# A kernel of attention and mixture of experts on one core: in VectorE's program for the experts, the part for units of one half block stands first behind the test of the unit's size

## The chip, the cores and the metric

The kernel runs on one core of a Trainium2 chip. The metric is the device time of one execution in microseconds (us); of several executions the median is taken. The engines are TensorE (PE in the profile, PEld for its weight loads), VectorE (DVE), ScalarE (ACT), GpSimd (POOL) and SyncE (SP), which here issues most of the DMAs. Each engine runs its own row of instructions; a "q" behind the name (DVEq) means the engine's sequencer, which takes branches and waits on semaphores.

## The reference

The first half is attention over keys and values averaged in groups of eight; the second half gives each of 4608 tokens to the one expert of eight that its gate likes best.

```python
def _attn_ref(q, k, v):                       # q, k, v: 8 x 8 heads x 576 x 64
    k_p = k.reshape(B, H, Sp, pool, D).mean(axis=3)
    v_p = v.reshape(B, H, Sp, pool, D).mean(axis=3)
    scores = scale * np.matmul(q, k_p.transpose(0, 1, 3, 2))
    ...
    return np.matmul(attn, v_p).astype(np.float32)

def _moe_ref(x, w_gate, w1, w2):              # x: 4608 x 512, w1: 8 x 512 x 1024, w2: 8 x 1024 x 512
    logits = x @ w_gate
    expert_idx = np.argmax(logits, axis=1)
    ...
    for e in range(E):
        mask = expert_idx == e
        xe = x[mask]
        h = np.maximum(xe @ w1[e], 0.0)
        out[mask] = gate_w[mask, None] * (h @ w2[e])
```

## The kernel before

Attention runs first and writes each token's row to a buffer of its expert in device memory. `plan` then works out a table from the counts of tokens. `experts` goes through that table unit by unit: a unit is up to 512 tokens of one expert, counted in half blocks of 64 tokens (`n`, 1 to 8, the table's column K_U). With the inputs at hand there are 13 units, 0 to 12, with 8, 8, 1, 6, 4, 8, 5, 8, 4, 1, 8, 8 and 6 half blocks. Units 2 and 9 have one half block. K_SW is 1 for a unit that begins a new expert, here for units 2, 3, 4, 5, 7, 9 and 10; the weights change there.

The matrix products are done in parts of high and low precision. ScalarE rounds an operand to the high part and VectorE takes the difference as the low part: `whi` (L1161) and `wlo` (L1169) for a piece of the weights W, eight pieces of 128x1024 per expert, 0 to 3 of W1 and 4 to 7 of W2, which SyncE loads into ST (L1427); `xhi` (L1123) and `xlo` (L1137) for the tokens X; `hhi` (L1059) and `hlo` (L1080) for the hidden values H, in eight groups f = 0 to 7 per unit. PE multiplies X with W1 in eight groups (L888) and H with W2 (L946).

A unit of one half block has its own form: PE multiplies with tokens as the fixed side (L913) and turns the result back (L924); ScalarE takes the rows (`htake`, L1038) and the high part (`hhi1`, L1048); VectorE sums halves (`hsums`, L1044) and takes the low part (`hlo1`, L1052), twice each (a = 0 and 1). PE's L946 for the first four k waits for `hlo1(u, 0)`, that for the last four for `hlo1(u, 1)`.

Nothing is scheduled by a tool in `experts`. Each engine's program is written out by hand for up to 16 units, with tests of `n` and of K_SW at run time; the engines meet at semaphores. For a unit VectorE runs `hidden_lo` (L1208 on: the low parts of H, with the W2 pieces between) and then `following`, which branches on `n` again (L1316, L1319); for one half block it runs `hlo1(u, 1)` and then, in `next_part` (test of K_SW at L1246), `xlo` and the W1 pieces of the next unit. After that come the unit's outputs Y (L1302 to L1308) and the table reads for the unit after the next (`keep`). The test values `n` and K_SW stand in registers that `keep` loaded a unit earlier.

SyncE loads for each unit, in this order: X of the unit after the next (L1392), its gates (L1384), the W2 pieces of the unit's expert to come (`stage(u, 1)`, L1427; after a unit of one or two half blocks only when PE has finished with its outputs, L1451), and the W1 pieces (`stage(u + 1, 0)`).

Of the kernel before, what the change touches and what calls it, by code (L numbers as in the profile page):

```python
# [47 lines left out]
K_U, K_SW, K_ROW, K_ST, K_AH, NK = 0, 1, 2, 6, 7, 8  # L48
# [3 lines left out]
def f32(a):  # L52
    return a.bitcast(F32)
# [684 lines left out]
def experts(ctx, tc, xs, w1v, w2v, out, tab, W, ident, empty, scr, u0, banks):  # L738
# [14 lines left out]
    pe, act, dve, sp, pool = nc.tensor, nc.scalar, nc.vector, nc.sync, nc.gpsimd  # L753

    with tc.tile_critical():
# [10 lines left out]
        def entry(eng, a, u, lo, hi):  # L766
            r = regs.get((eng, a, u))
            return eng.value_load(tab[u : u + 1, a : a + 1], min_val=lo, max_val=hi) if r is None else r
# [43 lines left out]
        def col(eng):  # L812
            c = next(cols[eng])
            return scr[:, c : c + 1]
# [5 lines left out]
        def vnop(n, v):  # L820
            dve.tensor_copy(out=col(dve), in_=scr[:, 0:1]).then_inc(Q[n], v)
# [76 lines left out]
        def tbank(u, a):  # L898
            return pH[(8 * u + (2, 0)[a]) % 3]

        def sums_h(u, a):

            return (hbank(u, 1) if a else pY[:, 0])[:, 0:256].rearrange("p (f t) -> p f t", f=4)
# [136 lines left out]
        def hsums(u, a):  # L1040
            dve.wait_ge(Q["P_h"], 8 * u + 4 + 4 * a)
            if a == 0:
                dve.wait_ge(Q["V_y"], 4 * u)
            dve.tensor_reduce(out=sums_h(u, a), in_=tbank(u, a).rearrange("p (f a t) -> p f t a", f=4, a=2), axis=AX.X, op=ALU.add).then_inc(Q["V_1"], 4)  # L1044
# [5 lines left out]
        def hlo1(u, a):  # L1050
            dve.wait_ge(Q["A_h"], 8 * u + 6 + 2 * a)
            dve.scalar_tensor_tensor(out=HH[:, 4 * a : 4 * a + 4, 64:128], in0=sums_h(u, a), scalar=0.0, in1=f32(HH[:, 4 * a : 4 * a + 4, 0:64]),  # L1052
                                     op0=ALU.max, op1=ALU.subtract).then_inc(Q["V_h"], 4)
# [109 lines left out]
        def wlo(u, i, other=None):  # L1163
            n, eng, q = "s1" if i < 4 else "s2", other or dve, "V_"
            eng.wait_ge(Q["A_" + n], 4 * (u - 1) + i % 4 + 1)
            if other:
                eng.wait_ge(Q[q + n], 4 * (u - 1) + i % 4)
            o = slice((i % 4) * 1024, (i % 4 + 1) * 1024)
            eng.tensor_tensor(out=(W1L if i < 4 else W2L)[:, o], in0=ST[:, i, :], in1=f32((W1H if i < 4 else W2H)[:, o]), op=ALU.subtract).then_inc(Q[q + n], 1)  # L1169

        def hidden(eng, u, part, wpart, nop, fs=range(8), small=False, turns=lambda: None):


            at = (0, 1, 3, 4) if small else (0, 1, 2, 3) if eng is act else (0, 2, 4, 6)
            for f in fs:
                part(f)
                if f == 5:
                    turns()
                if u > 0 and f in at:
                    with eng.If(entry(eng, K_SW, u, 0, 1) == 1):  # L1180
                        wpart(u, 4 + at.index(f))
                    if f == at[0]:
                        with eng.Else():
                            nop()
# [23 lines left out]
        def hidden_lo(u, fs=range(8), small=True):  # L1208
            go = lambda n, odd=None: hidden(dve, u, lambda f: hlo(u, f, n, odd), wlo, lambda: vnop("V_s2", 4), fs, n <= 2, turns if n > 2 and u > 0 else lambda: None)
            n = entry(dve, K_U, u, 1, 8)  # L1210

            def turns():
                more(dve, u + 1, lambda: [xturn(u + 1, s) for s in range(2)])

            def large():
                with dve.If(n % 2 == 0):
                    go(8)
                with dve.Else():
                    go(7, 64 * nc.s_assert_within(n, 1, 7, skip_runtime_bounds_check_because="an odd number of at most eight") - 64)

            if not small:
                return large()
            with dve.If(n > 2):
                large()
            with dve.Else():
                with dve.If(n > 1):
                    go(2)
                with dve.Else():
                    with dve.If(entry(dve, K_SW, u, 0, 1) == 1):
                        wlo(u, 4)  # L1230
                        wlo(u, 5)
                        hsums(u, 0)
                        wlo(u, 6)
                        hlo1(u, 0)
                        hsums(u, 1)
                        wlo(u, 7)
                    with dve.Else():
                        vnop("V_s2", 4)
                        hsums(u, 0)
                        hlo1(u, 0)  # L1240
                        hsums(u, 1)

        def next_part(eng, u, xf, xnop, wf, wnop, turn=None, mid=lambda: None, between=2, first=None):

# [47 lines left out]
        def dve_unit(u):  # L1292
# [58 lines left out]
            if u > 0:  # L1351
                hidden_lo(u)
# [317 lines left out]
```

## Time and profile before

| | |
|---|---|
| runs before | median 595.34 us (594.51 to 596.46, 3 runs) |
| profiled execution | 599.22 us, of which the span from the first to the last instruction is 597.6 us |
| mean granted clock of PE in it | 0.993 of full speed |
| busy, share of the span | PE 95%, DVE 62%, ACT 40%, POOL 29% |
| instructions in the trace of DVE | 738 |
| unit 2 | about 262 to 273 us |
| unit 9 | about 461 to 477 us |

The profiled execution is 3.9 us longer than the median of the runs. The granted clock is the rate that PE was given as a share of 2.4 GHz: 0.50 is 1.2 GHz. In the chain of work that ended last, "issue" is time in which an engine waited for nothing that the profile shows.

### The profile page before, as it was taken

The page shows a single profiled execution, that of the slowest core. Times are in us where ns is not written, and L with a number is a line of the kernel's source. Part 1 is how long each engine was busy: PE and PEld are TensorE (multiplying, and loading weights), DVE is VectorE, ACT ScalarE, POOL GpSimd, SP SyncE. Part 2 cuts the span into 40 slices and gives each one's busy share as a digit, 9 for nine tenths or more (in the row PEclk, how much of TensorE's full clock was granted, in tenths as well). Part 3 has the DMA queues.
Part 4 walks back from the last instruction along what each step waited for, and adds up shares of the span by engine and source line. Part 5 has one row for each costly group of instructions (what it writes and reads, how often), then busy time and mean ns, then how long its engine had stood idle before and what let it go on. Part 6 is the DMA issues. An engine that isn't in the chain of part 4 may idle for free.

```text
span 597.6 us, 13333 instructions
## 1 busy us (share of the span) xinstructions
PE 565.0 (95%) x4332; PEld 500.6 (84%) x4332; DVE 373.3 (62%) x738; ACT 240.7 (40%) x445; POOL 171.0 (29%) x250
## 2 busy tenths in 40 slices
PE   6988998999998999999998999999999799999995
PEld 5777987979877888888997889878898688888994
DVE  6698787888785223648959662786338768234221
ACT  2566675688531112346544420434125642021110
POOL 7456666556343111124211101030112220101101
PEclk9999999999999999999999999999999799999999
DMA  8979989797422557456685953044513542100101
GB/s 320 367 226 287 287 258 282 198 278 187 126 107 90 163 159 246 146 162 219 147 298 132 319 164 112 2 149 145 177 40 119 132 162 58 57 0 21 55 4 55
DMA packets 93946, 96.54 MB, mean 162 GB/s; under 512 B 43102, under 2 KB 74846, under 8 KB 93792
## 3 DMA queue, kind: packets, MB, share of 16 engines
q1 hardware_dynamic: 85808, 74.27, 43.4%
q0 software_dynamic: 7440, 20.50, 9.5%
q8 instruction: 60, 0.98, 0.7%
q14 instruction: 94, 0.77, 0.4%
q10 hardware_dynamic: 544, 0.02, 0.1%
HBM read 72.68 MB, written 26.00 MB: 165 GB/s over the span
## 4 chain that ended last, share of the span: by engine, by line
PE 66%; DVE 11%; issue 9%; SPq 4%; POOL 4%; DMA 3%; ACT 2%; DVEq 1%; POOLq 0%; ACTq 0%
PE pU L946 26%; PE pP L888 16%; PE pq L888 8%; PE pU L322 4%; PE pP L306 2%; DMA XE<-in_v_dram 2%; POOL dispatched L431 2%; PE pS L286 2%; PE pq L276 2%; PE pP L488 2%; DMA ST<-in_moe_w_dram 1%; DVE mx L290 1%; SPq L1392 1%; POOL raw L195 1%; SPq L1427 1%
## 5 line engine op out<-in xcount | busy, mean ns | idle before, releaser
L946 PE MATMUL pU<-W,H 128*128 128x512 f32 x912 | 203.7, 384 | 5.3 <-DVE H L1052 3.2
L946 PEld LDWEIGHTS pU<-W,H 128*128 128x128 f32 x912 | 173.4, 191 | 31.9 <-DVE H L1052 3.4
L1504 POOL DMA_INDIRECT out_dram<-Y,GT x51 | 55.6, 1091 | 308.2 <-DVE Y L1308 226.7
L888 PE MATMUL pP<-X,W 128*128 128x512 f32 (+3 forms) x660 | 122.0, 340 | 3.8 <-DVEq L1544 1.5
L888 PEld LDWEIGHTS pP<-X,W 128*128 128x128 f32 x660 | 108.4, 190 | 14.1 <-issue 3.3
L1059 ACT ACTIVATE H<-pP 128x512 fp32r<-128x512 f32 x56 | 33.4, 597 | 143.4 <-PE pP L888 135.4
L1308 DVE TENSOR_SCALAR Y<-pU,GT 128x512 f32<-128x512 f32 x36 | 26.8, 749 | 86.6 <-PE pU L946 78.7
L1080 DVE SCALAR_TENSOR_TENSOR H<-pP,H 128x512 fp32r<-128x512 f32 (+1 forms) x62 | 39.9, 643 | 53.9 <-ACT H L1059 50.6
L1169 DVE TENSOR_TENSOR W<-ST,W 128x1024 fp32r<-128x1024 f32 x54 | 64.2, 1213 | 9.0 <-ACT W L1161 8.5
L1161 ACT CAST W<-ST 128x1024 fp32r<-128x1024 f32 x56 | 56.8, 1051 | 27.1 <-PE pU L946 20.0
L888 PE MATMUL pq<-X,W 128*128 128x512 f32 (+3 forms) x324 | 62.4, 342 | 0.0
L322 PE MATMUL pU<-V,pt 110*128 110x146 f32 (+3 forms) x468 | 56.7, 283 | 1.4 <-ACT pt L307 0.8
L888 PEld LDWEIGHTS pq<-X,W 128*128 128x128 f32 x324 | 53.8, 190 | 5.0 <-issue 0.2
L322 PEld LDWEIGHTS pU<-V,pt 110*128 110x128 f32 (+3 forms) x468 | 51.4, 179 | 3.1 <-ACT pt L307 1.6
L431 POOL DMA_INDIRECT dispatched<-xe,ix x36 | 39.8, 1105 | 17.2 <-POOL ix L392 7.3
L1059 ACT ACTIVATE H<-pq 128x512 fp32r<-128x512 f32 x28 | 16.7, 598 | 61.1 <-PE pq L888 60.0
L1132 DVE STREAM_TRANSPOSE pS<-XE 128x512 f32<-128x512 f32 x26 | 38.0, 1503 | 0.0
L307 ACT COPY pt<-pP 110x384 f32<-110x384 f32 x72 | 30.7, 479 | 6.1 <-PE pP L306 5.7
L290 DVE TENSOR_REDUCE mx<-pS 128x8 f32<-128x576 f32 x36 | 27.1, 753 | 9.2 <-PE pS L286 4.4
L1080 DVE SCALAR_TENSOR_TENSOR H<-pq,H 128x512 fp32r<-128x512 f32 (+1 forms) x30 | 19.6, 655 | 20.5 <-ACT H L1059 19.5
L299 ACT ACTIVATE P<-sd 128x576 f32<-128x576 f32 x36 | 24.8, 689 | 17.8 <-DVE sd L293 16.1
L306 PE MATMUL pP<-ident,P 128*110 128x128 f32 x216 | 30.0, 275 | 0.6 <-ACT P L299 0.6
(205 smaller groups left out, 610.9 us busy)
## 6 DMA issues: line engine op xcount, KB each, us to landing
ST<-in_moe_w_dram SPq DMA_DIRECT2D x56, 512.0 KB
raw<-in_k_dram SPq DMA_DIRECT2D x12, 768.0 KB
raw<-in_v_dram SPq DMA_DIRECT2D x11, 768.0 KB
XE<-dispatched SPq DMA_DIRECT2D x104, 64.0 KB, 2.2
qa<-in_q_dram SPq DMA_DIRECT2D x24, 256.0 KB
w<-in_moe_w_dram SPq DMA_DIRECT2D x8, 512.0 KB
XE<-dispatched SPq DMA_DIRECT2D x15, 256.0 KB, 4.0
qa<-in_q_dram SPq DMA_DIRECT2D x2, 1024.0 KB
```

The costliest lines, as they stand in the source:

```text
L290: nc.vector.tensor_reduce(out=mx, in_=s4, axis=AX.X, op=ALU.max)
L306: nc.tensor.transpose(pPs[a][0:R, c * P : (c + 1) * P], Ps[t % 2][:, o : o + R], ident)
L322: nc.tensor.matmul(pu[p0 : p0 + n, a, h * VW : (h + m) * VW], lhsT=pt[t][a][0:r, c % 3 * P + p0 : c % 3 * P + p0 + n], rhs=Vs[g % 2][0:r, ...
L431: apart(nc.gpsimd.indirect_dma_start(out=xs, out_offset=bass.IndirectOffsetOnAxis(ap=at, axis=0), in_=rows, in_offset=None))
L888: r = pe.matmul(out=pH[g % 3][:, :m], lhsT=w1s(w, f, k), rhs=x, start=i == 0, stop=i == len(passes) - 1)
L946: r = pe.matmul(out=pY[:, s % 2, :], lhsT=h, rhs=in_turn(w[:, k * 512 : (k + 1) * 512]), start=start and i == 0, stop=stop and i == len(ps ...
L1059: act.activation(out=HH[:, f, o], in_=src[:, o], func=AF.Relu).then_inc(Q["A_h"], 1)
L1080: return dve.scalar_tensor_tensor(out=dst[:, f, to], in0=src[:, at], scalar=0.0, in1=f32(HH[:, f, at]), op0=ALU.max, op1=ALU.subtract)
L1132: dve.transpose(out=pX[:, s % 2, :].rearrange("p (c a g t) -> p c g t a", c=4, a=2, g=4), in_=XE[u % 2][:, s, :].rearrange("p (g r c) -> p ...
L1161: act.copy(out=(W1H if i < 4 else W2H)[:, o], in_=ST[:, i, :]).then_inc(Q["A_s1" if i < 4 else "A_s2"], 1)
L1169: eng.tensor_tensor(out=(W1L if i < 4 else W2L)[:, o], in0=ST[:, i, :], in1=f32((W1H if i < 4 else W2H)[:, o]), op=ALU.subtract).then_inc( ...
L1504: pool.indirect_dma_start(out=out, out_offset=bass.IndirectOffsetOnAxis(ap=GT[:, u, s, 1:2].bitcast(I32), axis=0), in_=Y[:, s, :], in_offs ...
```

## The change

In `hidden_lo` the two tests of the unit's size change places. Before, `n > 2` is tested first (L1223), the larger units' part stands behind it, then the part for two half blocks (test L1226), then that for one half block (test of K_SW at L1229). After, `n < 2` is tested first (L1223), with the one-half-block part directly behind it (test of K_SW at L1224), and then `n > 2` (L1238), the larger units' part and the part for two half blocks. The parts themselves are the same, and so are the programs of the other engines. VectorE's program has 6697 built instructions in both.

```diff
-            with dve.If(n > 2):
-                large()
+            with dve.If(n < 2):
+                with dve.If(entry(dve, K_SW, u, 0, 1) == 1):
+                    wlo(u, 4)
+                    wlo(u, 5)
+                    hsums(u, 0)
+                    wlo(u, 6)
+                    hlo1(u, 0)
+                    hsums(u, 1)
+                    wlo(u, 7)
+                with dve.Else():
+                    vnop("V_s2", 4)
+                    hsums(u, 0)
+                    hlo1(u, 0)
+                    hsums(u, 1)
             with dve.Else():
-                with dve.If(n > 1):
+                with dve.If(n > 2):
+                    large()
+                with dve.Else():
                     go(2)
-                with dve.Else():
-                    with dve.If(entry(dve, K_SW, u, 0, 1) == 1):
-                        wlo(u, 4)
...
-                    with dve.Else():
-                        vnop("V_s2", 4)
...
```

VectorE's row for unit 9 before, at the end of the parts for larger units, where the one-half-block part begins (L1064 and L1080 belong to the part for two half blocks):

```order
L1080 SCALAR_TENSOR_TENSOR H<-pP_65,H 128x128
L1080 SCALAR_TENSOR_TENSOR H<-pP_66,H 128x128
L1226 UNCONDITIONAL_BRANCH
L1229 COMPARE_AND_BRANCH
L1169 TENSOR_TENSOR W<-ST,W 128x1024 x2
L1044 TENSOR_REDUCE pU<-pq 128x256
L1169 TENSOR_TENSOR W<-ST,W 128x1024
L1052 SCALAR_TENSOR_TENSOR H<-pU,H 128x4x64
L1044 TENSOR_REDUCE pP_66<-pP_65 128x256
L1169 TENSOR_TENSOR W<-ST,W 128x1024
L1229 UNCONDITIONAL_BRANCH
```

VectorE's row for unit 9 after, from the end of unit 8 (L1367; L783 is the test whether there is a unit 9) through the test of the size:

```order
L1367 UNCONDITIONAL_BRANCH
L783 COMPARE_AND_BRANCH
L1223 COMPARE_AND_BRANCH
L1224 COMPARE_AND_BRANCH
L1169 TENSOR_TENSOR W<-ST,W 128x1024 x2
L1044 TENSOR_REDUCE pU<-pq 128x256
L1169 TENSOR_TENSOR W<-ST,W 128x1024
L1052 SCALAR_TENSOR_TENSOR H<-pU,H 128x4x64
L1044 TENSOR_REDUCE pP_66<-pP_65 128x256
L1169 TENSOR_TENSOR W<-ST,W 128x1024
L1224 UNCONDITIONAL_BRANCH
```

The one-half-block part has moved from 108 rows behind the test L1223 to the row directly behind it, ahead of the larger units' part (some 86 built instructions) and of that for two half blocks (some 31). Its end branch was a few rows ahead of the join; it now passes both other parts.

VectorE's row for unit 2 after, at the join behind `hidden_lo`, where `following` begins (before, the first three rows are the end of the one-half-block part):

```order
L1064 TENSOR_REDUCE pq<-pq 128x128
L1080 SCALAR_TENSOR_TENSOR H<-pP_66,H 128x128
L1080 SCALAR_TENSOR_TENSOR H<-pq,H 128x128
L1240 UNCONDITIONAL_BRANCH
L1316 COMPARE_AND_BRANCH
L1246 COMPARE_AND_BRANCH
L1137 TENSOR_TENSOR X<-pS,X 128x8x64 x2
```

VectorE's row for unit 2 further on, in both kernels at the same place: the part of `following` for one half block, which L1316 and L1319 lead to (L1249 ends the part for two half blocks).

```order
L1169 TENSOR_TENSOR W<-ST,W 128x1024 x4
L1249 UNCONDITIONAL_BRANCH
L1052 SCALAR_TENSOR_TENSOR H<-pq,H 128x4x64
L1246 COMPARE_AND_BRANCH
L1137 TENSOR_TENSOR X<-pS,X 128x8x64 x2
L1112 COMPARE_AND_BRANCH
L1137 TENSOR_TENSOR X<-pm,X 128x8x64
```

Nothing moved between L1316, L1319 (91 rows behind L1316) and these rows (34 behind L1319); what changed is where VectorE comes from: before, from six rows ahead of L1316 in unit 2, after, from 109 rows ahead of it.

## Rows read from the trace of the kernel before

**Rows 1.** The page of the profiled execution, whole program: the span, the busy line of the engines, the granted clock in 40 slices, and the DMA queue of kind instruction (packets, MB, share).

```profile
span 597.6 us, 13333 instructions
...
PE 565.0 (95%) x4332; PEld 500.6 (84%) x4332; DVE 373.3 (62%) x738; ACT 240.7 (40%) x445; POOL 171.0 (29%) x250
...
PEclk9999999999999999999999999999999799999999
...
q14 instruction: 94, 0.77, 0.4%
```

**Rows 2.** What PE's queue waited for: the first row from 455 us to the end, the other two from 262 to 460 us. Columns: engine, line, what was waited for, us in total, times, longest us.

```profile
PE pU L946 <- DVE H L1052: 3.2, 1, 3.2
...
PE pP L888 <- DVE X L1137: 1.4, 1, 1.4
...
PE pU L946 <- DVE W L1169: 0.5, 1, 0.5
```

**Rows 3.** The chain of work that ended last, 455 to 490 us, through unit 9. Columns: start us, duration us, what (DVEq is VectorE's sequencer).

```profile
461.32 0.06 DVEq L1223
...
461.52 0.06 DVEq L1226
461.58 4.61 issue
...
466.20 0.05 DVEq L1229
...
466.30 0.13 DVE W L1169
...
470.02 0.05 DVEq L1229
...
470.79 6.51 PE pU L946 x16
```

**Rows 4.** Stretches of 2 us: busy time of each engine, then PE's granted clock, the DMA share and GB/s.

```profile
458.00:460.00 2.00, 2.00 (x11) 1.76 (x10) 2.00 (x3) 0.00 (x0) 0.00 (x0) 1.00 0.94 302
...
468.00:470.00 2.00, 0.00 (x0) 0.00 (x0) 2.00 (x3) 0.38 (x1) 0.00 (x0) 0.91 0.35 67
...
470.00:472.00 2.00, 1.21 (x3) 1.04 (x4) 2.00 (x4) 1.81 (x4) 0.20 (x1) 0.50 0.46 112
...
474.00:476.00 2.00, 2.00 (x6) 1.62 (x5) 2.00 (x3) 2.00 (x3) 0.72 (x1) 0.50 0.37 81
...
476.00:478.00 2.00, 2.00 (x10) 1.66 (x9) 2.00 (x3) 0.29 (x1) 0.00 (x0) 0.88 0.17 14
...
266.00:268.00 2.00, 1.98 (x17) 1.74 (x16) 1.93 (x3) 2.00 (x5) 0.00 (x0) 1.00 0.12 41
```

**Rows 5.** VectorE's branches by line, the first five in unit 2 (261 to 274 us), the last at the start of a later unit (288 to 294 us). Columns: line, operation, count, duration in ns, first and last start in us.

```profile
L1226 DVEq COMPARE_BRANCH  x1: 62/62/62, 262.5 to 262.5; - x1
...
L1229 DVEq COMPARE_BRANCH  x2: 47/48/50, 262.6 to 267.5; - x2
...
L1316 DVEq COMPARE_BRANCH  x1: 56/56/56, 267.7 to 267.7; - x1
...
L1319 DVEq COMPARE_BRANCH  x1: 56/56/56, 268.2 to 268.2; - x1
...
L1246 DVEq COMPARE_BRANCH  x1: 56/56/56, 268.8 to 268.8; - x1
...
L1246 DVEq COMPARE_BRANCH  x1: 63/63/63, 290.3 to 290.3; - x1
```

**Rows 6.** VectorE's line of time, 268 to 273.2 us (unit 2) and 288 to 294 us (the last row). Columns: start us, us, engine, line, operation, what, count, and in brackets the idle time before it and what ended it.

```profile
269.22 0.42 DVE L1052 SCALAR_TENSOR_TENSOR H<-pq,H 128x256 fp32r<-128x256 f32 x1
...
270.68 1.29 DVE L1137 TENSOR_TENSOR X<-pS,X 128x512 fp32r<-128x512 f32 x2 [1.04 <-ACT scr L818]
...
272.49 0.14 DVE L821 COPY scr<-scr 128x1 f32<-128x1 f32 x1
...
292.90 1.29 DVE L1137 TENSOR_TENSOR X<-pS,X 128x512 fp32r<-128x512 f32 x2 [0.24 <-issue]
```

**Rows 7.** Lines of time around unit 9's end and unit 10, columns as in rows 6: PE's last transposes of unit 9's stretch, ScalarE's first casts of it, SyncE's loads, then ScalarE, VectorE and PE at unit 10's fifth group.

```profile
466.96 0.65 PE L840 MATMUL pU<-ident,XE 128*128 128x128 f32 x4
...
461.01 1.99 ACT L1161 CAST W<-ST 128x1024 fp32r<-128x1024 f32 x2 [4.62 <-PE pU L946]
...
464.55 10.06 SPq L1392 DMA_DIRECT2D XE<-dispatched  x16
475.26 2.75 SPq L1384 DMA_DIRECT2D GT<-dispatched  x4
480.75 2.92 SPq L1427 DMA_DIRECT2D ST<-in_moe_w_dram  x4
...
484.46 1.04 ACT L1161 CAST W<-ST 128x1024 fp32r<-128x1024 f32 x1 [3.94 <-DMA ST<-in_moe_w_dram]
...
486.68 0.68 DVE L1080 SCALAR_TENSOR_TENSOR H<-pP,H 128x512 fp32r<-128x512 f32 x1
...
487.49 2.78 PE L888 MATMUL pP<-X,W 128*128 128x512 f32 x12
```

**Rows 8.** The chain of work that ended last, 476 us to the end. Columns as in rows 3.

```profile
575.81 15.55 PE pU L946 x72
591.36 0.02 issue
```

More of the change, by code (lines that the diff above doesn't have):

```diff
@@ L1222, in hidden_lo @@
                 return large()
-            with dve.If(n > 2):
-                large()
+            with dve.If(n < 2):
[12 more added lines that the diff above has]
+                    hsums(u, 1)
             with dve.Else():
-                with dve.If(n > 1):
+                with dve.If(n > 2):
+                    large()
+                with dve.Else():
                     go(2)
-                with dve.Else():
-                    with dve.If(entry(dve, K_SW, u, 0, 1) == 1):
-                        wlo(u, 4)
[L1231 to L1236, printed above, removed]
-                    with dve.Else():
-                        vnop("V_s2", 4)
-                        hsums(u, 0)
-                        hlo1(u, 0)
-                        hsums(u, 1)
         def next_part(eng, u, xf, xnop, wf, wnop, turn=None, mid=lambda: None, between=2, first=None):
```

## The prediction

> **What bounds the kernel.** The page gives TensorE (PE) 95% busy in a span of 597.6 us and the clock near full almost everywhere [rows 1]. So a change on VectorE (DVE) counts only where PE waits for it, or where PE's waiting takes its clock down. I read PE's waits next, for the two stretches that hold the one-half-block units: unit 2 (about 262 to 273 us) and unit 9 (461 to 477 us). After 455 us PE waits once, 3.2 us for H of line 1052, which is `hlo1` of unit 9; its waits from 262 to 460 are small ones for DVE, the longest 1.4 us [rows 2]. The other units take the branch to a larger part, before and after.
>
> The chain through unit 9 shows what `hlo1` was late for [rows 3]: DVE runs the tests L1223 and L1226 within 0.2 us, and then nothing until L1229, 4.61 us later, called "issue". L1229 is a branch on a register that was loaded a unit earlier; it waits for no semaphore. What can be late is the instruction itself. PE's last transposes end at 467.6; it then stands until 470.79 [rows 3, 7]. The stretches show what followed [rows 4]: the granted clock is 0.91 in 468–470, 0.50 in 470–476 (1.2 GHz), 0.88 in 476–478. PE's 16 matmuls L946 take 6.51 us [rows 3]; at full clock 72 of them take 15.55 us [rows 8], so 16 take 3.46. Unit 9 thus loses about 3.2 us to the wait and up to 3.05 us to the clock.
>
> In unit 2 the same jump, L1226 to L1229, shows no hole (262.5 to 262.6 [rows 5]), so the distance alone costs nothing; whether the code is already there decides. It is late elsewhere too [rows 5, 6]: L1246 runs at 290.3 and the L1137 behind it not before 292.90, 2.6 us later, put down to "issue"; in unit 2 L1319 runs at 268.2, L1246 at 268.8, and L1137 at 270.68, after 1.04 us idle put down to a ScalarE copy, 2.45 us behind L1319. My reading: DVE's code comes in pieces (94 packets of kind instruction, 0.77 MB on one queue, 8.2 KB each [rows 1]), one piece is asked for when DVE enters the one before it, and it takes 2.4 to 2.9 us, or 4 to 5.3 us where the DMA share is near 1 (0.94 in 458–460, against 0.12 in 266–268 [rows 4]). Counting built instructions, I place the edges 128 instructions apart; that count is inference, the holes are rows.
>
> The Trainium skill, page "Runtime: NRT & Kernel Launch", section "Instruction fetch mechanics", says that prefetch is sequential and normally hidden, and that a taken branch to a target outside a two-line window stalls on a fetch. By that rule only far jumps stall; the trace disagrees, since 290.3 to 292.90 is a step to the next piece with no far jump, and by the rule the change would cost unit 2 nothing.
>
> **The change, step by step.**
>
> *Larger units.* One more branch, L1238, jumps over some 21 instructions. Near branches stand 0.2 us apart [rows 3]; ten units times 0.2 us lie on DVE's sequencer while PE works ahead, so 0 on the path; 0.2 us each at each of the two waits for DVE shown in [rows 2] where a larger unit begins, if the cover is gone: 0.4 us at most.
>
> *Where the small part lies now.* It stands directly behind L1223, in the piece already there: no hole at its start. But its end jump L1224 now passes the larger parts (some 126 instructions) into the next piece, and L1316, two branches later, jumps on to L1319, into the piece behind, which is asked for only then. The hole moves from ahead of the small part to behind it, ahead of `hlo1(u, 1)` and of `xlo`, the low half of the next unit's X.
>
> *Unit 2* had no hole ahead of the small part, so it can only lose. The part itself is held by W pieces and by PE's transposes and ends where it did, about 267.5. L1316 comes at about 268.0, after the jump into a ready piece (0.5 us, as from L1316 to L1319 before). L1319 waits for its piece, 2.45 us: 270.5, was 268.2. `hlo1` follows at about 270.8, was 269.22; the next piece is asked for at 270.5 and `xlo` starts at 273.0, was 270.68: +2.35. From `xlo` to PE's next unit the chain is DVE's own (L1137, L821 at 272.49 [rows 6], PE next), so unit 3 starts 2.35 us late. Behind it PE waits 1.4 and 0.5 us for DVE [rows 2]; these waits end by the same late chain, so I let them absorb 0.3. Unit 2: +2.05 us. Bounds: 0 if the piece is hidden, 2.8 if both fetches take 2.9 us and nothing absorbs.
>
> *Unit 9* gets rid of the 4.61 us. The small part starts when ScalarE has rounded W2's first piece, about 462.1 (the first of two casts from 461.01 [rows 7]), instead of 466.30; its W pieces, sums and `hlo1(9, 0)` keep their spacing (3.7 us from 466.30 to the end branch at 470.02 [rows 3], plus waits for PE's transposes), so it ends at about 466.7 and L1316 runs at 467.3. Now L1319's piece is asked for at about 467, with the DMA share down to 0.35 in 468–470 [rows 4]: 2.5 to 3 us, 469.8. `hlo1(9, 1)` runs at about 470.1 to 470.8; `xlo` at 470.5 to 473.2. PE starts L946 at 467.6 with two pauses of about 1 us and no fall of the clock, and reaches unit 10 at about 473.7 instead of 477.1: −3.4 us. Bounds: 0 if the new fetch takes 5.3 us, −4.2 without a second hole.
>
> *What unit 10 does with it* is where I expect the gain to go. PE's fifth group of unit 10 starts at 487.49, directly behind DVE's H at 486.68, which takes up what ScalarE's H writes behind ScalarE's W at 484.46; that W had waited 3.94 us for a W2 load [rows 7]. The load belongs to four that SyncE issues from 480.75 on, in its own sequence: behind 16 loads of X from 464.55 and the gate loads from 475.26, with table reads between [rows 7]; from 461 to 489 the waits of SyncE's queue show none. ScalarE takes its instructions in order, so its H for the fifth group stands behind that W piece. With unit 10 begun 3.4 us earlier, PE finishes its first four groups at 484.1 and stands until about 487.45: 3.4 back to 0. That pause is as long as the one in unit 9 before, behind which the clock stayed at 0.50 until about 476.5, 5.7 us after PE's restart; the same in unit 10 costs 2.8 us of work. Bounds 0 to 2.8; I take 2.1, nearer to the row, since whatever lengthens unit 9's second hole shortens this pause. From there PE runs without a pause to 591.4 [rows 8], so what is lost stays lost. If the W2 load is not what holds the fifth group, the 3.4 us stay.
>
> Sum: unit 2 +2.05, unit 9 −3.4, unit 10 +3.4 +2.1, larger units 0: +4.1 us. The profiled execution took 599.2 us (span 597.6 and 1.6 around it), 3.9 above the median of the runs, 595.34; differences carry over, so 595.3 + 4.1 = 599.4 us.
>
> **Rivals.**
>
> *PE waits in unit 10, but the clock stays up.* 595.3 + 2.05 = 597.4. For it: PE pauses of up to 1.4 us left the clock alone; against it: the pause expected is 3.3 us, as in unit 9.
>
> *The clock falls in unit 2 too.* There PE would stand twice, about 1.3 and 1.9 us, around eight matmuls. The only fall in the rows came about 2 us into a pause. It adds up to 2.8: 602.0.
>
> *The new holes are hidden.* If VectorE's code is always there one piece and more ahead, and only the 4.61 us were a far jump's, unit 2 loses nothing, unit 9 gains, unit 10 takes the gain back. Without a clock loss 595.3; with it 597.4. The holes behind 290.3 and 268.8 speak against it. This is what the rule of the Trainium skill's page above would make of the change.
>
> *Not slower: unit 10 isn't held.* If DVE and ScalarE, coming earlier, have the fifth group's H ready without that W2 piece (or SyncE's loads come earlier with the unit), PE keeps the 3.4 us: 595.3 + 2.05 − 3.4 = 594.0, and under 593.5 where unit 2 loses less than 1.6. It decides from the point where ScalarE's W leaves 484.46: if that moves with unit 10, this case holds. Against it: SyncE's order depends on none of what moves.
>
> **Chances.** About 0.3%, 1.8 us, is what a measurement of this kernel can tell from no change. Forecast (599.4, from 598 to 600.3): 0.46. No clock loss in unit 10 (597.4): 0.18. Clock falls in unit 2 too (602): 0.08. Holes hidden (595.3 to 597.4): 0.13. Unit 10 not held (594.0): 0.15. Slower by over 0.3% (above 597.1): the first and third whole, two thirds of the second, under a third of the fourth: 0.68. Faster (under 593.5): 0.10, half of the last case and some of the fourth. Same: 0.22. The range from 593.6 to 600.8 leaves out the case with two clock losses, the better half of the last, and the upper edge of the forecast's. The forecast's own range is 598.0 to 600.3.
>
> **What would show it.** In the changed profile the hole L1223 to L1224 in unit 9 is gone; L1316 to L1319 shows 2.4 us or more in units 2 and 9; unit 2's L1137 comes 5.0 us behind L1316 (3.0 before), and PE waits some 2 us there; the clock row has its low slice in unit 10, not in unit 9; ScalarE's W still waits for a W2 load at unit 10's fifth group. If L1319 follows L1316 by 0.5 us in unit 2, the piece count is wrong; if the low slice is gone altogether, the clock term is.

## The result and the profile after

The changed kernel takes 600.77 us (median of 6 runs, 600.0 to 602.19) against 596.53 us for the kernel before, in the same comparison: ratio 1.0077, 95% interval 1.0053 to 1.0100. That is 4.6 us, 3.2 to 6.0. A second comparison gave 601.42 us and 1.0092 (1.0061 to 1.0123), 5.5 us. The forecast was +4.1 us and 599.4, from 598.0 to 600.3; both measured times lie above that range, the first just inside the wider one that ends at 600.8. As a difference +4.1 lies inside both intervals (3.2 to 6.0 and 3.6 to 7.3 us). The kernel before took 1.2 us more in this comparison than the 595.34 that the forecast was built on.

The page of the profiled execution of after, to be laid beside [rows 1]:

```profile
span 598.3 us, 13341 instructions
...
PEclk9999999999999999999999999999999989999999
```

The low slice of the granted clock has moved one place to the right, from the end of unit 9 to unit 10. What PE's queue waited for, the first three rows from 262 to 460 us, the other two from 455 us to the end (columns as in [rows 2]):

```profile
PE pP L888 <- DVE W L1169: 3.0, 1, 3.0
PE pP L888 <- DVE scr L821: 1.7, 1, 1.7
PE pU L946 <- DVE H L1052: 1.4, 1, 1.4
...
PE pP L888 <- DVE H L1080: 3.5, 1, 3.5
PE pU L946 <- DVE H L1052: 2.1, 1, 2.1
```

Before, there were 3.2 us for `hlo1` of unit 9 and little else. Now `hlo1` costs 1.4 us in unit 2 and 2.1 in unit 9, the start of unit 3 another 1.7, the start of unit 5 3.0 (1.4 before) and the fifth group of unit 10 3.5. VectorE's branches, the first three in unit 2, the other four in unit 9 (columns as in [rows 5]):

```profile
L1224 DVEq COMPARE_BRANCH  x1: 47/47/47, 261.6 to 261.6; - x1
...
L1316 DVEq COMPARE_BRANCH  x1: 56/56/56, 262.1 to 262.1; - x1
...
L1319 DVEq COMPARE_BRANCH  x1: 56/56/56, 264.7 to 264.7; - x1
...
L1223 DVEq COMPARE_BRANCH  x1: 43/43/43, 459.2 to 459.2; - x1
...
L1224 DVEq COMPARE_BRANCH  x2: 43/45/47, 459.3 to 464.6; - x2
...
L1316 DVEq COMPARE_BRANCH  x1: 63/63/63, 465.2 to 465.2; - x1
...
L1319 DVEq COMPARE_BRANCH  x1: 63/63/63, 467.6 to 467.6; - x1
```

In unit 9 the test of K_SW (L1224) follows L1223 in 0.1 us, where before 4.61 us passed ahead of it [rows 3]. In both units L1319 now stands 2.4 to 2.6 us behind L1316, where it was 0.5. VectorE's line of time in unit 2 (columns as in [rows 6]):

```profile
264.99 0.42 DVE L1052 SCALAR_TENSOR_TENSOR H<-pq,H 128x256 fp32r<-128x256 f32 x1 [1.58 <-issue]
267.14 1.29 DVE L1137 TENSOR_TENSOR X<-pS,X 128x512 fp32r<-128x512 f32 x2 [1.73 <-issue]
...
268.95 0.14 DVE L821 COPY scr<-scr 128x1 f32<-128x1 f32 x1
```

`hlo1` and `xlo` each stand behind a hole put down to "issue". L1137 comes 5.0 us behind L1316, 3.0 before [rows 5, 6]. In unit 10 (SyncE, ScalarE and PE, lines of time; answers to [rows 7]):

```profile
462.71 11.32 SPq L1392 DMA_DIRECT2D XE<-dispatched  x16
...
479.25 2.70 SPq L1427 DMA_DIRECT2D ST<-in_moe_w_dram  x4
...
483.46 1.04 ACT L1161 CAST W<-ST 128x1024 fp32r<-128x1024 f32 x1 [7.67 <-DMA ST<-in_moe_w_dram]
...
472.33 2.83 PE L888 MATMUL pq<-X,W 128*128 128x512 f32 x12 [1.06 <-DVE W L1169]
...
486.42 7.13 PE L888 MATMUL pP<-X,W 128*128 128x512 f32 x24 [3.49 <-DVE H L1080]
```

PE's fifth group waits 3.49 us for the H that stands behind ScalarE's W, which waited for the W2 load issued at 479.25. Stretches of 2 us behind it (columns as in [rows 4]):

```profile
484.00:486.00 2.00, 0.00 (x0) 0.00 (x0) 1.47 (x2) 1.90 (x3) 0.00 (x0) 1.00 1.02 391
486.00:488.00 2.00, 1.58 (x7) 1.38 (x8) 1.69 (x3) 2.00 (x5) 0.00 (x0) 0.94 0.44 169
488.00:490.00 2.00, 2.00 (x7) 1.53 (x6) 1.09 (x2) 1.00 (x2) 0.00 (x0) 0.50 0.47 101
490.00:492.00 2.00, 2.00 (x8) 1.68 (x7) 0.71 (x2) 0.60 (x1) 0.00 (x0) 0.71 0.55 125
```

The clock falls to 0.50 here as it did in unit 9 before: the 24 matmuls of L888 take 7.13 us instead of 5.34.

To see where the time went, the executions are cut where PE starts on a unit (its first L913 or L888, or the first L946 of unit 10), two traces of each kernel. For the first trace of before these starts are 192.14, 261.55, 272.73, 327.69, 460.75, 477.13 and 497.88 us, and PE ends at 591.35; for the first of after 185.93, 255.65, 269.19, 325.65, 458.64, 472.33, 498.57 and 592.03. Us:

| stretch | before | before, again | after | after, again | mean difference | forecast |
|---|---|---|---|---|---|---|
| units 0 and 1 | 69.41 | 69.74 | 69.72 | 69.36 | 0.0 | 0 |
| unit 2 | 11.18 | 12.30 | 13.54 | 14.13 | +2.1 | +2.35 |
| units 3 and 4 | 54.96 | 54.17 | 56.46 | 54.14 | +0.7 | −0.3 |
| units 5 to 8 | 133.06 | 133.09 | 132.99 | 134.16 | +0.5 | 0 |
| unit 9 | 16.38 | 15.92 | 13.69 | 12.38 | −3.1 | −3.4 |
| unit 10, to its first L946 | 20.75 | 21.70 | 26.24 | 28.84 | +6.3 | +5.5 |
| the rest | 93.47 | 93.47 | 93.46 | 93.46 | 0.0 | 0 |
| sum | 399.21 | 400.39 | 406.10 | 406.47 | +6.5 | +4.1 |

The first L888 of unit 0 starts at 192.14 us in the first trace of before and between 185.9 and 187.2 in the other three: attention and the plan differ by that much between executions of one code. The stretches behind them differ too, by 1.2 us in sum between the two traces of before. So four traces and the medians agree only to about 2 us.

### The profile page after: what moved, and what is told of

It reads as the page before. It is cut to its first block, busy times and chain, and to the rows that moved or that the text cites. A ratio compares the mean times of both kernels' runs of the same rounds, so it can differ in the third digit from the quotient of the medians.

```text
span 598.3 us, 13341 instructions
## 1 busy us (share of the span) xinstructions
PE 564.2 (94%) x4332; PEld 499.9 (84%) x4332; DVE 372.3 (62%) x738; ACT 240.6 (40%) x445; POOL 171.3 (29%) x250
## 4 chain that ended last, share of the span: by engine, by line
PE 67%; DVE 15%; issue 6%; SPq 3%; DMA 3%; ACT 2%; DVEq 2%; POOL 1%; POOLq 0%; ACTq 0%
PE pU L946 27%; PE pP L888 17%; PE pq L888 8%; PE pU L322 4%; PE pP L306 2%; DMA XE<-in_v_dram 2%; DVE mx L290 2%; PE pS L286 2%; DVE sd L293 2%; PE pP L488 2%; SPq L1392 2%; DVE raw L195 2%; DVE W L1169 2%; PE pm L230 1%; PE pq L276 1%
## 5 line engine op out<-in xcount | busy, mean ns | idle before, releaser
L946 PE MATMUL pU<-W,H 128*128 128x512 f32 x912 | 201.4, 380 | 5.1 <-DVE H L1052 3.5
L946 PEld LDWEIGHTS pU<-W,H 128*128 128x128 f32 x912 | 171.2, 189 | 31.5 <-issue 5.4
L888 PE MATMUL pP<-X,W 128*128 128x512 f32 (+3 forms) x660 | 123.7, 344 | 9.8 <-DVE H L1080 3.7
L888 PEld LDWEIGHTS pP<-X,W 128*128 128x128 f32 x660 | 109.6, 191 | 20.9 <-issue 5.4
L1080 DVE SCALAR_TENSOR_TENSOR H<-pP,H 128x512 fp32r<-128x512 f32 (+1 forms) x62 | 39.9, 643 | 56.3 <-ACT H L1059 54.5
L888 PE MATMUL pq<-X,W 128*128 128x512 f32 (+3 forms) x324 | 62.5, 343 | 1.2 <-DVE W L1169 1.1
L888 PEld LDWEIGHTS pq<-X,W 128*128 128x128 f32 x324 | 53.7, 190 | 6.7 <-issue 1.9
L1080 DVE SCALAR_TENSOR_TENSOR H<-pq,H 128x512 fp32r<-128x512 f32 (+1 forms) x30 | 19.6, 654 | 20.3 <-ACT H L1059 19.7
L195 POOL TENSOR_TENSOR raw<-raw 128x768 f32<-128x768 f32 (+1 forms) x18 | 27.1, 1504 | 10.9 <-DMA raw<-in_v_dram 10.2
```

The lines of the kernel that those rows point to most:

```text
L195: return lambda: eng.tensor_tensor(out=out, in0=raw[:, :, 0:n], in1=raw[:, :, n : 2 * n], op=ALU.add)
L888: r = pe.matmul(out=pH[g % 3][:, :m], lhsT=w1s(w, f, k), rhs=x, start=i == 0, stop=i == len(passes) - 1)
L946: r = pe.matmul(out=pY[:, s % 2, :], lhsT=h, rhs=in_turn(w[:, k * 512 : (k + 1) * 512]), start=start and i == 0, stop=stop and i == len(ps ...
L1080: return dve.scalar_tensor_tensor(out=dst[:, f, to], in0=src[:, at], scalar=0.0, in1=f32(HH[:, f, at]), op0=ALU.max, op1=ALU.subtract)
```

## The experiments

The theory: VectorE's code comes in pieces of 128 instructions, one asked for ahead, so that the change moves a hole from ahead of unit 9's small part to behind both small parts; unit 2 pays, and what unit 9 gains unit 10 gives back behind a late W2 load, with the clock on top. The rivals: the loss is unit 2's alone; the holes belong to one execution; unit 10 is held by VectorE's or ScalarE's work. Ratios are to the kernel before in the same comparison. Some of the kernels have a few lines more, so that L946 is L947 there, L888 is L889, L1316 is L1332.

**The two units apart.** In the first run the new order stands in unit 9 alone, in the second in unit 2 alone:

```diff
-            with dve.If(n < 2):
-                ...
+            if u in FIRST:        # (9,) in the first run, (2,) in the second
+                with dve.If(n < 2):
+                    ...           # the order of the change
+            else:
+                with dve.If(n > 2):
+                    ...           # the order of before
```

> The order of the change for unit 9 alone; every other unit as before. Theory (code comes in pieces; unit 2 and unit 9 pay apart): unit 2 is as before, L1316 to L1319 stands 0.5 us apart there; unit 9 has no hole ahead of its small part and a new one of about 2.4 us between L1316 and L1319; unit 10 starts about 2.7 us earlier against unit 9's first transposes, PE then waits about 3.5 us for the fifth group's H behind a W2 load, the clock falls there, and the end is 2 to 3 us later than before: ratio 1.003 to 1.005. Rival (the loss is all unit 2's): ratio 0.995 to 1.000.

> The order of the change for unit 2 alone. Theory: L1316 to L1319 takes about 2.5 us in unit 2 instead of 0.5, L1137 starts about 2.4 us later against PE's transposes, unit 3 starts 2.35 us late; unit 9 is as before with its 4.6 us hole and the low clock behind it. Ratio 1.003 to 1.006 (2 to 3.8 us: the upper end if PE's wait of 3.0 us ahead of unit 5 comes with it). Rival (the new holes come from how attention's end falls in a run, not from the order): L1319 0.5 us behind L1316, ratio 1.000.

Unit 9 alone: 1.0034 (1.0005 to 1.0062), 2.0 us. Unit 2 alone: 1.0045 (1.0021 to 1.0068), 2.7 us. Together 4.7, the change 4.6, with intervals of 1.4 to 1.7 us to either side of each. So both pay, and nothing else has to. VectorE's branches in unit 2, new order there (these lines are L1316 and L1319 of before):

```profile
L1332 DVEq COMPARE_BRANCH  x1: 63/63/63, 262.5 to 262.5; - x1
...
L1335 DVEq COMPARE_BRANCH  x1: 62/62/62, 265.2 to 265.2; - x1
```

The hole is 2.7 us; unit 2 takes 13.60 us. In unit 9 alone, PE's line of time:

```profile
482.89 5.45 PE L889 MATMUL pP<-X,W 128*128 128x512 f32 x24 [0.62 <-DVE H L1081]
```

Unit 9 takes 14.12 us instead of 16.38, as expected, but in this trace the fifth group waits only 0.62 us and unit 10, begun at 471.54, takes 21.81 us, not 25 or more. SyncE's W2 loads left at 475.95 here, 4.4 us behind the unit's start, in the trace of after 6.9 us behind it; the 16 loads of X ahead of them took 9.27 us to issue here and 11.32 there. What unit 10 gives back depends on when SyncE gets to these loads, and that varies; the measured 2.0 us is the answer over 12 runs. Unit 2 took 13.15 us in this trace though its order is that of before; PE stood 1.8 us ahead of L946 there, "issue", of which more below.

**The W2 loads first.** The third run is the changed kernel with SyncE's order turned in unit 9, the sixth the kernel before with the same, the fifth the new order in unit 9 alone with it:

```diff
             def following():
...
+                if u in (9,):
+                    stage(u, 1)
+                    rows()
+                    return stage(u + 1, 0)
                 rows()
                 if u > 0:
                     stage(u, 1)
```

> The changed kernel, and SyncE issues in unit 9 the W2 loads for unit 10 ahead of the X loads for unit 11. Theory (unit 10's fifth group is held by the W2 load that SyncE issues late): the loads leave at about 473 instead of 479 us, PE's wait of 3.5 us in unit 10 and the low clock behind it are gone; 4 to 5 us less than the changed kernel, ratio to before 0.998 to 1.003. Rival (the group is held by VectorE's or ScalarE's own work, the load is only the last name): PE still waits over 2 us there, ratio 1.006 to 1.010.

> The order of the change for unit 9 alone, and in unit 9 SyncE's W2 loads for unit 10 ahead of the X loads for unit 11. Theory (unit 9's part of the change gains about 3 us, the late W2 load takes them back): unit 10 starts 3 us earlier against the start of unit 9 and PE no longer waits at its fifth group; 2 to 4.5 us less than before, ratio 0.993 to 0.997. Rival (unit 9 gains nothing in most executions): ratio 0.998 to 1.003.

> The kernel before, with SyncE's W2 loads of unit 9 ahead of the X loads for unit 11 and nothing else. Theory (before, unit 10's fifth group was only just held by the load): no difference beyond 1 us, ratio 0.998 to 1.002, PE reaches unit 10 as before, 20.5 to 21 us from its start to its first L946. Rival (the order of loads alone is worth what the third experiment gained): ratio 0.990 to 0.994.

| | SyncE as before | W2 loads first in unit 9 |
|---|---|---|
| order of before | 1 | 0.9976 (0.9954 to 0.9999) |
| new order in unit 9 | 1.0034 (1.0005 to 1.0062) | 0.9939 (0.9920 to 0.9959) |
| new order everywhere | 1.0077 (1.0053 to 1.0100) | 0.9990 (0.9965 to 1.0015) |

The new order in unit 9 loses 0.34% with SyncE as before and gains 0.37% (0.9976 to 0.9939) with the loads moved. This is the point on which the rival "unit 10 isn't held" turned, and it is settled: the W2 load is what holds unit 10. SyncE and PE in the third run:

```profile
473.60 2.89 SPq L1427 DMA_DIRECT2D ST<-in_moe_w_dram  x4
480.20 8.49 SPq L1392 DMA_DIRECT2D XE<-dispatched  x16
...
484.10 5.34 PE L888 MATMUL pP<-X,W 128*128 128x512 f32 x24
```

The loads leave at 473.60 and PE goes through unit 10, begun at 473.66, without a wait, 20.79 us to its first L946; the stretches from 484 on show the clock at 1.00. The load order alone was worth a little more than expected, 1.4 us where I had allowed 1. The kernel before had something to gain there: in the four traces with unit 9 and SyncE as before unit 10 takes 20.75 to 22.03 us, and in three of them its fifth group waits 0.3 to 1.0 us for the same H; in all five with the loads moved it takes 20.7 to 20.8. The fifth run takes 592.39 us against 595.62 and is 0.6% faster than the kernel before, the lowest ratio in this study (the eleventh run's lies inside its interval). PE in its unit 9 and unit 10:

```profile
465.72 2.83 PE L947 MATMUL pU<-W,H 128*128 128x512 f32 x12 [1.83 <-issue]
469.11 2.83 PE L889 MATMUL pq<-X,W 128*128 128x512 f32 x12 [0.56 <-issue]
...
479.55 5.34 PE L889 MATMUL pP<-X,W 128*128 128x512 f32 x24
```

**One piece more in the jump.** In the fourth run 128 instructions that no unit here executes stand in unit 2's part for two half blocks, in the kernel before:

```diff
                     with dve.If(n > 1):
                         go(2)
+                        for _ in range(128 if u == 2 else 0):
+                            dve.drain()
```

> The kernel before with 128 instructions, one piece, put into unit 2's part for two half blocks, which no unit here runs: nothing more is executed, the code behind keeps its place against the pieces' edges, and the jump from L1226 to L1229 in unit 2 is one piece longer. Theory (only the next piece is asked for ahead): a hole of 2.4 to 3 us between L1226 and L1229 in unit 2, where it was 0.2; unit 3 starts 2 to 2.5 us late, ratio 1.003 to 1.005. Rival (code is there two pieces ahead, or the jump is what costs nothing at any length): no hole, ratio 1.000.

VectorE's small part of unit 2, and PE behind it:

```profile
260.11 2.36 DVE L1170 TENSOR_TENSOR W<-ST,W 128x1024 fp32r<-128x1024 f32 x2 [2.69 <-issue]
...
264.60 5.42 PE L947 MATMUL pU<-W,H 128*128 128x512 f32 x16 [1.56 <-DVE H L1053]
269.85 4.06 PE L889 MATMUL pP<-X,W 128*128 128x384 f32 x24
```

The hole is there, 2.69 us ahead of the first W piece; before there was none [rows 5]. PE waits 1.56 us for `hlo1`, the granted clock falls behind the wait (0.78, 0.50 and 0.87 in 264–270), and unit 2 takes 13.38 us instead of 11.18 and 12.30. Yet the time is 1.0003 (0.9982 to 1.0024), below the 1.003 expected: in the trace the part behind attention is 401.54 us long, 1.7 more than the mean of the two traces of before, of which unit 2 is 1.6, but the 12 runs leave room for no more than 1.4 us. The place of the hole is shown, its price in the whole is not.

That the holes are code which comes late can be read from the traces themselves, for they time every packet of queue q14 [rows 1], 8192 bytes each. Here one ends at 258.55 and L1229 of before runs at 260.01, 1.5 us later. In unit 2 of the changed kernel packets end at 263.32 and 265.78; L1319 and `xlo` follow 1.4 us behind them. In unit 9 before, one ends at 464.60 and L1229 follows 1.6 us behind. In these holes of unit 2 the packet starts 0.6 to 0.9 us behind the last branch. In unit 9 it starts 2.7 to 2.8 us behind L1226 in five traces with VectorE's order of before there (both of before, second, fourth and sixth run): this is where the two extra microseconds of that hole lie. The DMA share was 0.85 to 0.99 meanwhile, so the prediction's reading, that the traffic makes it late, fits but isn't shown. Traffic is not needed: at 577 us, with the share at 0.06, the jump from L783 to L1328 took 3.5 us before, and its packet started 1.6 us behind L783.

**The distance undone, the order kept.** In the tenth run unit 2 has the new order, but the parts for larger units that the end branch passes are left out there (unit 2 doesn't run them):

```diff
             with dve.If(n < 2):
                 ...
             with dve.Else():
-                with dve.If(n > 2):
-                    large()
-                with dve.Else():
-                    go(2)
+                for _ in range(3):
+                    dve.drain()
```

> Unit 2 alone has the order of the change, and the parts for larger units that its end branch passes are left out there (unit 2 doesn't run them), so the join lies in the same piece as the small part; all code behind stands 101 instructions nearer. Theory: L1316's test follows the end branch at once, the next test 0.5 us behind; the piece of hlo1 is asked for only then, so one hole of 2 to 2.5 us stands ahead of hlo1, at about where PE's wait starts, and none ahead of X: X starts 0 to 0.5 us later than before against the unit's start, where the change alone gave 2.4. Rival (the order costs unit 2 its 2.4 us by something other than distance): X 2 us late or more. The total is not to be read: the pieces' edges move for all units behind.

VectorE's line of time in unit 2:

```profile
271.62 0.42 DVE L1052 SCALAR_TENSOR_TENSOR H<-pq,H 128x256 fp32r<-128x256 f32 x1 [1.38 <-issue]
271.96 1.28 DVE L1137 TENSOR_TENSOR X<-pS,X 128x512 fp32r<-128x512 f32 x2
```

One hole ahead of `hlo1`, which runs 2.4 us behind the branch before it, and none ahead of X. Against PE's first L913 of the unit (262.58 here, 261.55 before) X starts 0.25 us later than before, in the changed kernel 2.36 later (267.14 behind 255.65). The order as such costs unit 2's X nothing; what lies between its end and what follows does. (The run moves the pieces' edges together with the distance, so it doesn't part these two. PE did not profit in full, unit 2 took 12.59 us: its L946 stood 1.5 us at "issue". The ratio of the whole, 1.0063, is not to be read: all code behind has moved against the edges, and unit 10 took 26.21 us in the trace.)

Unit 9 of this run parts the jump from the place. It has the order of before there, with the same parts to pass, but all its code stands 101 instructions nearer. From the test that is L1226 before to that which is L1229 (462.96 and 463.87) 0.9 us pass, not 4.7, and unit 9 takes 14.07 us. So the hole ahead of its small part comes from where that code lies, not from the order of the tests or the length of the jump.

**No jump at all.** In the ninth run the hidden part, `hlo1`, X and the W1 pieces stand in one row behind the test in units 2 and 9, in the eleventh in unit 9 alone, both with the W2 loads first:

```diff
+                with dve.If(n < 2):
+                    hidden_lo(u, only="one")
+                    hlo1(u, 1)
+                    more(dve, u + 1, lambda: part(True, first=lambda: None))
+                    early()
+                with dve.Else():
+                    hidden_lo(u, only="rest")
+                    more(dve, u + 1, larger, early)
```

> In units 2 and 9 VectorE's whole way for one half block (hidden part, hlo1, X and W1 pieces of the next unit) stands in one row behind the test of the size, so that no jump lies between the small part and X; the other parts stand behind it; SyncE's W2 loads of unit 9 go first. Theory (pieces of 128, one asked for ahead): no hole ahead of the small parts, hlo1 or X; one hole of 2.4 to 3 us behind the W1 pieces, ahead of Y and of the next unit's first low part of H. Unit 9: unit 10 starts 5 to 6 us earlier against unit 9's start than before. Unit 2: unit 3 starts about 1.3 us earlier, but PE waits about 2 us for its first H, so 0 to +1 in all. Ratio 0.987 to 0.994. Rival (holes come wherever a unit of one half block ends, whatever the distance): ratio as for unit 9 alone, 0.994, with holes ahead of X.

> As the run with both units joined, for unit 9 alone; unit 2 as before. Theory: no hole ahead of unit 9's small part, hlo1 or X, unit 10 starts 5 to 6 us earlier against unit 9's start than before, the hole ahead of Y and unit 10's first H costs PE nothing or up to 1 us; ratio 0.987 to 0.992, 1 to 2.5 us better than the order of the change for unit 9 with the loads moved (0.994). Rival (unit 10 is held by something else as soon as it starts earlier): 0.994.

VectorE in unit 2 of the ninth run:

```profile
269.10 0.42 DVE L1052 SCALAR_TENSOR_TENSOR H<-pq,H 128x256 fp32r<-128x256 f32 x1
269.43 1.28 DVE L1137 TENSOR_TENSOR X<-pS,X 128x512 fp32r<-128x512 f32 x2
...
279.03 0.15 DVE L821 COPY scr<-scr 128x1 f32<-128x1 f32 x1 [3.90 <-issue]
```

No hole ahead of `hlo1` and X any more, but one of 3.90 us ahead of the outputs, where the row now jumps over the other parts. It makes unit 3's first H late: PE waits 3.3 us for it. Nor does unit 3 start earlier: unit 2 takes 11.34 us, and 11.18 and 12.30 before. The ratio is 1.0055 (1.0026 to 1.0085), not 0.987 to 0.994. Unit 3's H is part of that; the stretch of units 3 and 4 took 61.52 us, with two more waits of PE at "issue" (2.7 and 2.0 us) around the start of unit 5. I had priced the new hole, with what unit 2 gains, at 0 to 1 us. In unit 9 of the eleventh run, VectorE and PE:

```profile
467.61 0.42 DVE L1052 SCALAR_TENSOR_TENSOR H<-pP,H 128x256 fp32r<-128x256 f32 x1
467.94 1.28 DVE L1137 TENSOR_TENSOR X<-pS,X 128x512 fp32r<-128x512 f32 x2
...
476.74 0.15 DVE L821 COPY scr<-scr 128x1 f32<-128x1 f32 x1 [2.86 <-issue]
...
469.23 2.83 PE L946 MATMUL pU<-W,H 128*128 128x512 f32 x12 [1.57 <-issue]
```

The hole ahead of the outputs is 2.86 us and costs PE nothing, as expected: unit 10 needs its first H late. But PE's L946 does not start with `hlo1`, done at 468.03; it stands until 469.23 at "issue". Unit 9 takes 12.55 us, against 12.93 in the fifth run: 3.8 less than in the first trace of before, not 5 to 6. The ratio is 0.9945 (0.9920 to 0.9970), the rival's number. With VectorE's hole gone, PE's own row is the next limit in unit 9.

**Both kernels once more.**

> The changed kernel once more, for a second trace. Theory: ratio 1.005 to 1.010; unit 3 starts 2.3 to 2.8 us later against the first unit than before, unit 10 takes over 3 us longer than before up to its first L946; if the 1.5 us lost between units 3 and 5 came from how one execution's loads fell, they are another number here, if from the change, the same.

> The kernel before once more, for a second trace and as a measure of what equal kernels differ by: ratio 0.998 to 1.002. Theory: the hole of 4 to 5 us ahead of unit 9's small part and the low clock are there again, none ahead of unit 2's. Rival (the hole belongs to that one execution): under 1 us.

After: 1.0092. ScalarE's W and PE in its unit 10:

```profile
484.07 1.04 ACT L1161 CAST W<-ST 128x1024 fp32r<-128x1024 f32 x1 [9.55 <-DMA ST<-in_moe_w_dram]
...
487.03 7.86 PE L888 MATMUL pP<-X,W 128*128 128x512 f32 x24 [5.37 <-DVE H L1080]
```

Unit 9 gained more here (12.38 us) and the pause became 5.37 us, the 24 matmuls behind it 7.86. The 1.5 us between units 3 and 5 were gone (54.14). In unit 2 the clock fell (PE, then stretches with columns as in [rows 4]):

```profile
266.03 4.52 PE L946 MATMUL pU<-W,H 128*128 128x512 f32 x12 [2.14 <-DVE H L1052]
...
266.00:268.00 2.00, 1.97 (x6) 1.68 (x7) 0.39 (x1) 1.27 (x2) 0.24 (x1) 0.66 0.04 8
268.00:270.00 2.00, 2.00 (x6) 1.55 (x6) 2.00 (x5) 0.00 (x0) 0.00 (x0) 0.50 0.05 12
```

Before: 0.9993 (0.9972 to 1.0015). VectorE's branches in its units 2 and 9, and one of PE's waits in unit 2:

```profile
L1226 DVEq COMPARE_BRANCH  x1: 62/62/62, 257.5 to 257.5; - x1
...
L1229 DVEq COMPARE_BRANCH  x2: 47/48/50, 257.7 to 262.9; - x2
...
L1226 DVEq COMPARE_BRANCH  x1: 63/63/63, 457.2 to 457.2; - x1
...
L1229 DVEq COMPARE_BRANCH  x2: 47/48/50, 462.0 to 465.9; - x2
...
PE pU L946 <- issue: 1.5, 1, 1.5
```

0.2 us from L1226 to L1229 in unit 2, 4.8 us in unit 9: the hole belongs to the place, not to the execution. But in unit 2 PE stood 1.5 us at "issue", and the unit took 12.30 us instead of 11.18. That wait runs beside VectorE's and covers part of what the change costs there: over the six traces that have the order and the code of before in unit 2, it takes 11.2 to 13.2 us, in the mean 12.0, and over the four with the new order 13.5 to 14.1, in the mean 13.7. That is 1.7 us more.

## Why most steps of the prediction held and its time was too low

The hole ahead of unit 9's small part went, as forecast, and the new hole between L1316 and L1319 came where it was put, with the forecast's length: 2.4 to 2.7 us for 2.45. Unit 3 started 2.1 us late in the mean of the table, 1.7 over all traces, for a forecast of 2.35. The hidden-holes rival is out by the rows of after. By the rule of the Trainium skill's page "Runtime: NRT & Kernel Launch", section "Instruction fetch mechanics", a taken branch stalls when its target lies outside a two-line window. The tenth run speaks against so wide a window, since there the jump over 34 rows from the test that is L1319 before to `hlo1` still left a hole.

The time failed first by its base. *"Differences carry over, so 595.3 + 4.1"* took the median of three runs of the kernel before; over six it is 596.53, and these 1.2 us are most of the 1.4 us between 599.4 and 600.77. In the sum itself two terms were mis-sized and one was left out.

*"I let them absorb 0.3"* behind unit 2. Nothing was absorbed: +0.7 us in the mean, +1.9 in one trace and −0.4 in the other, against the mean of before. In the first trace of after (SyncE, PE, and VectorE's X around the start of unit 5):

```profile
317.49 9.16 SPq L1427 DMA_DIRECT2D ST<-in_moe_w_dram  x8
...
325.65 2.83 PE L888 MATMUL pP<-X,W 128*128 128x512 f32 x12 [2.95 <-DVE W L1169]
...
322.36 1.28 DVE L1137 TENSOR_TENSOR X<-pS,X 128x512 fp32r<-128x512 f32 x2
```

PE's unit 5 starts at 325.65, though X was done at 323.64; the name "DVE W" is only the last event ahead of it. The traces time the packets of the other queue of kind instruction, q8, too, 16,384 bytes each: one ends here at 323.76, and PE starts 1.9 us behind it. Each of PE's eleven waits of over 1 us at "issue" in units 2, 5 and 9 and at the end of unit 4, in all traces, ends 1.5 to 1.9 us behind such a packet. So it is PE's own code that was late. Unit 5's eight W loads left 48.3 us behind unit 3's start (317.49 against 269.19). Over all 13 traces the stretch of units 3 and 4 is long where they leave early: 56.46, 56.63 and 61.52 us where they leave 46.9 to 48.4 us behind, 55.21 at 49.3, and 54.1 to 55.0 in the nine traces with 50 to 52.4. The kernels with the new order in unit 2 tend to be the early ones, presumably because PE and VectorE move by 2 us there and SyncE by less. That the loads delay PE's code fits this, but no run separated it, so the cause of this term stays open.

*"3.4 back to 0, and 2.1 for the clock."* The place and the load were right, but the load did not stay where it was: it left 20.6 and 20.8 us behind unit 9's start instead of 20.0 (20.5 in the second trace of before), and ScalarE's W started 4.2 and 4.6 us behind it instead of 3.7. The pause was 3.5 and 5.4 us, the clock's part 1.8 and 2.5 us (7.13 and 7.86 less 5.34): unit 10 cost 6.3 us in the mean for a forecast of 5.5. "SyncE's order depends on none of what moves" was true of the order and wrong of the times. That the clock's part came out near the 2.1 chosen between 0 and 2.8 was partly luck: the same wait of 3.2 us in unit 9 cost the clock 3.05 us in the one trace that the forecast had and about 2.2 in the second trace of before.

*The clock in unit 2* was put at nothing in the sum and left to a rival with a chance of 0.08. In the first trace of after it stayed at 1.00 there, behind waits of 1.4 and 1.7 us. In the second it fell behind a wait of 2.14 us, and 12 matmuls took 4.52 us instead of 2.83. So the rival came true in one of two executions. It cost less than the 2.8 us set for it, since `xlo` was late meanwhile and PE then waited for it no more: unit 2 took 14.13 us against 13.54.

Together the first two terms miss 1.8 us. The 0.5 us in units 5 to 8 come from one trace, where PE waits 0.88 us for a W1 piece at the start of unit 7; the sixth run, with VectorE's order of before, shows the same wait, 1.1 us, so it isn't the change's own. By the traces the change costs 6.5 us, by the medians 4.6 and 5.5; the difference lies within what executions of one kernel vary, and the intervals of the runs leave room for +4.1.

## What to carry to other kernels

Where an engine's program is long and branches at run time, count what lies between the end of a part and what comes next on its path, not only what lies ahead of the part: moving a rarely taken part forward moves its jump behind it. Whether a jump then waits depends on where its target lies: 101 instructions fewer ahead of unit 9 took its hole away (tenth run). Before speeding up one stage, look at what the next stage waits for in the engines that do not move, here a load queued behind sixteen others, and move that first; the same edit went from +0.34% to −0.37%. And a pause that only changes its place can take the clock's fall with it, as in unit 10, but not each pause does, so a fall is better put into a sum with a chance than as a case apart.

## What the runs showed of the hardware

A branch to code that VectorE did not yet have waited 2.4 to 2.7 us in units 2 and 9, and 4.6 to 4.8 us ahead of unit 9's small part before; the longer jump of the ninth and eleventh runs left VectorE idle for 3.90 and 2.86 us. Of a hole of 2.4 to 2.7 us the code's packet takes 0.3 to 0.6, and 1.3 to 1.6 pass from its end to the late instruction. PE has such waits as well: 1.2 to 2.3 us at "issue" ahead of L946 in unit 2 or 9 of eight traces, the second of before (1.49) among them. I had not expected PE's own row to be next in line. The granted clock fell about 2 us into unit 9's pause before; in the changed kernel PE paused from 482.9 to 486.4, the stretch 484–486 still shows 1.00 and 486–488 shows 0.94, so the fall came as PE was at work again. In the second trace of after it fell some 3.5 us into unit 10's pause. The time from a pause's start to the fall is not one number. Nor did a pause's length decide whether the clock fell. It fell behind 1.56 us (fourth run, unit 2), 2.14 us (second trace of after, unit 2) and 2.26 us (first run, unit 9: 0.63 and 0.51 in 468–472), and stayed at 1.00 behind 2.08 us (after, unit 9), 2.95 us (after, unit 5) and 3.30 us (ninth run, unit 3).
